# The up projection by seven block products in tiles of 512 tokens, with every transform ahead of the feed-forward

## The chip, the cores and the metric

One Trainium2 chip, one NeuronCore. The metric is the device time of one execution in microseconds. TensorE (PE) multiplies, VectorE (DVE), ScalarE (ACT) and GpSimd (POOL) work on its results, SyncE (SP) issues nearly all transfers.

## What is computed

```
def _attn_ref(x, w_r, w_i, b_r, b_i):          # x: 8 x 3072 x 256
    X = np.fft.rfft(x, axis=1)
    Yr = Xr @ w_r - Xi @ w_i + b_r
    Yi = Xr @ w_i + Xi @ w_r + b_i
    Yr, Yi = soft-shrink by 0.01
    return np.fft.irfft(Yr + 1j * Yi, n=3072, axis=1)

def _moe_ref(x, w_in, w_out):                  # 24576 x 256, 256 x 2048, 2048 x 256
    h = x @ w_in
    g = np.where(h >= 1, h, np.where(h <= -1, 0, (h + 1) ** 2 / 4))
    return g @ w_out
```

The weights of the feed-forward come as float64; all else is float32. To keep float32's accuracy with the faster matmul format (F32R), an operand is held as two rounded parts, hi and lo, and a product is three matmuls: hi x hi, lo x hi, hi x lo.

## The kernel before

The transform of length 3072 = 48 x 64 is done as matmuls in four stages. The first stage runs over "halves" of x (96 partitions x 2 columns of j x 256 channels, 128 of them): load_x, split_x_hi (ACT), split_x_lo (DVE), stage1 (three matmuls of 512 columns), store_z to a DRAM scratch. The second stage, the mixing of channels and the inverse's first stage run over 96 "units" of two frequency groups (12 per batch): load_z, stage2, split_X, planes, mix (24 matmuls of 256 columns), shrink, split_Y, stage3 (12 matmuls of 256 columns), store_u to a second DRAM scratch. The inverse's last stage, load_u and stage4 (L309), writes y transposed (channels on the partitions) as yth and ytl.

The feed-forward runs over 64 tiles of 384 tokens and 16 blocks of 128 hidden channels, 1024 steps. up (L324) is six matmuls of 384 columns (two halves of the channels, three parts each) into one PSUM bank; then the gate: ACT's Relu r (L329), DVE's min and multiply (L331) and max (L333). split_g makes gh on ACT (L340) and gl on DVE (L341). down (L357) follows three steps later, nine matmuls of 256 columns that add into two PSUM banks over a tile's 16 steps; after a tile's last one ot is copied and stored.

The order is written out by hand (manual_schedule): each engine runs its instructions in program order. First come 22 halves, then a loop over the units of six batches with the first stage's halves and the weight conversion spread through it (weight_steps: float64 bits to two parts, on DVE, ACT and POOL). The feed-forward then starts, and the 24 units of the last two batches run between its steps, one every eight steps (the list `extra`). stage4 of the next tile runs after steps 3 and 11 of a tile.

```
        for n in range(N + DELTA):
            if n < N:
                up(n)
            if 1 <= n <= N:
                split_g(n - 1)
            for e, a in extra.get(n, ()):
                e(*a)
            if i + 1 < NX and f in (3, 11):
                stage4(i + 1, 0 if f == 3 else 1)
            if n >= DELTA:
                down(n - DELTA)
```

Of the kernel before, what the change touches and what calls it, by code (L numbers as in the profile page):

```python
# [71 lines left out]
def round_r(a):  # L72
    """To 11 mantissa bits, nearest even."""
# [21 lines left out]
def tile_fft_mix_moe(  # L95
# [9 lines left out]
    TOK = JT * Q  # L105
    NS = TOK // P
    NU = G // 2
    DELTA = 3

    const = ctx.enter_context(tc.tile_pool(name="const", bufs=1))  # L110
    work = ctx.enter_context(tc.tile_pool(name="work", bufs=2))
    psum = ctx.enter_context(tc.tile_pool(name="psum", bufs=2, space=bass.MemoryType.PSUM))
    dram = ctx.enter_context(tc.tile_pool(name="dram", bufs=1, space=bass.MemoryType.DRAM))

    xv = x.rearrange("b (q j) d -> b q j d", j=J)
    ov = out.rearrange("(b t r j) e -> b j r t e", b=B, t=NS, j=J)
# [21 lines left out]
    xin, xs, zst = {}, {}, {}  # L138
    HT = JT // 2
# [323 lines left out]
    with tc.manual_schedule():  # L463
# [48 lines left out]
        for u in range(U1):  # L512
# [5 lines left out]
            if u >= 3:  # L518
                store_u(u - 3)
# [121 lines left out]
```

## Time and profile before

| | |
|---|---|
| median of 3 runs | 2840.24 us (2839.85 to 2841.37) |
| span of the profiled execution | 2840.5 us |
| PE busy | 2816.6 us, 99% |
| DVE busy | 2140.1 us, 75% |
| ACT busy | 1464.3 us, 52% |
| POOL busy | 139.7 us, 5% |
| up products begin | at 440.7 us |

The profile shows one execution. Busy time is the time in which an engine has an instruction under way; matmuls overlap, so their cost is read from start to start of neighbours and not from their length. The chain that ended last follows the work back from the last instruction, at each step to what released it. A row of the timeline is one instruction (or some alike in a row): start, length, engine, line, operation, tiles and shapes, and in brackets how long its engine was idle before it and what ended that.

### The profile page before, as it was taken

To read this page: it belongs to the slowest core of one execution; us is meant where nothing else is said; L and a number is where in the kernel's file an instruction comes from. 1 tells how busy PE (TensorE), PEld (TensorE's weight loads), DVE (VectorE), ACT (ScalarE), POOL (GpSimd) and SP (SyncE) were. 2 spreads that over 40 slices of the span, in tenths; PEclk is the share of its full clock that TensorE was granted. 3 is DMA by queue.
4 is the path that set the end of the run, shared out by engine and by line. 5 is a ranking of instruction groups with operands and counts; after the bars stand their busy time and mean duration, and the time that the engine had idled before them with its cause. 6 is when DMAs were issued, how large, how long until landed. Compare 5 with 4: busy or idle time off the path is not lost.

```text
span 2840.5 us, 53099 instructions
## 1 busy us (share of the span) xinstructions
PE 2816.6 (99%) x20416; PEld 2774.8 (98%) x20416; DVE 2140.1 (75%) x4084; ACT 1464.3 (52%) x3034; POOL 139.7 (5%) x137
## 2 busy tenths in 40 slices
PE   7999999999999999999999999999999999999999
PEld 5999999999999999999999999999999999999999
DVE  5898987777777777777777777777777777777776
ACT  5777775554454444444444444444444444444444
POOL 0333330000000000000000000000000000000000
PEclk9999999999999999999999999999999999999999
DMA  8877772211111000000000000000000000000000
GB/s 250 253 218 214 219 208 90 67 47 43 40 40 53 29 22 23 23 23 23 23 23 23 23 23 23 23 23 23 23 23 23 24 23 23 23 23 23 23 24 18
DMA packets 110009, 168.43 MB, mean 59 GB/s; under 512 B 11099, under 2 KB 85691, under 8 KB 109755
## 3 DMA queue, kind: packets, MB, share of 16 engines
q1 hardware_dynamic: 108554, 161.82, 18.9%
q8 instruction: 160, 2.62, 0.4%
q0 software_dynamic: 1200, 3.22, 0.4%
q14 instruction: 95, 0.77, 0.1%
HBM read 89.50 MB, written 75.50 MB: 58 GB/s over the span
## 4 chain that ended last, share of the span: by engine, by line
PE 95%; DVE 3%; ACT 1%; DMA 1%; issue 1%; ACTq 0%; DVEq 0%; SPq 0%; POOLq 0%
PE acc L357 38%; PE ps_h L324 38%; PE ps_mix L242 8%; PE ps_i L309 4%; PE ps_f L169 3%; PE ps_f L190 2%; PE ps_i L277 2%; DVE xl L159 1%; DVE yl L268 1%; ACT xh L154 1%; DVE Xl L208 0%; DMA z_d<-zst 0%; ACT Xh L207 0%; ACT ust L285 0%; DMA c_sb<-in_c 0%
## 5 line engine op out<-in xcount | busy, mean ns | idle before, releaser
L329 ACT ACTIVATE r<-ps_h,half 128x384 f32<-128x384 f32 x1024 | 595.5, 582 | 1169.2 <-PE ps_h L324 1152.7
L331 DVE SCALAR_TENSOR_TENSOR sq<-r 128x384 f32<-128x384 f32 x1024 | 571.5, 558 | 568.6 <-ACT r L329 558.2
L357 PE MATMUL acc<-wouth,gh 128*128 128x256 f32 x3072 | 872.3, 284 | 0.0
L357 PE MATMUL acc<-wouth,gl 128*128 128x256 f32 x3072 | 864.2, 281 | 0.0
L357 PE MATMUL acc<-woutl,gh 128*128 128x256 f32 x3072 | 859.1, 280 | 0.0
L324 PE MATMUL ps_h<-yth,winl 128*128 128x384 f32 x2048 | 692.1, 338 | 0.0
L324 PE MATMUL ps_h<-yth,winh 128*128 128x384 f32 x2048 | 690.4, 337 | 0.4 <-ACT yth L311 0.4
L324 PE MATMUL ps_h<-ytl,winh 128*128 128x384 f32 x2048 | 690.0, 337 | 0.1
L333 DVE TENSOR_TENSOR g<-ps_h,sq 128x384 f32<-128x384 f32 x1024 | 570.9, 558 | 35.6
L357 PEld LDWEIGHTS acc<-wouth,gh 128*128 128x128 f32 x3072 | 578.6, 188 | 0.8
L357 PEld LDWEIGHTS acc<-woutl,gh 128*128 128x128 f32 x3072 | 577.5, 188 | 0.5
L357 PEld LDWEIGHTS acc<-wouth,gl 128*128 128x128 f32 x3072 | 577.2, 188 | 0.2 <-DVE gl L341 0.2
L341 DVE TENSOR_TENSOR gl<-g,gh 128x384 fp32r<-128x384 f32 x1024 | 561.5, 548 | 0.2 <-ACT gh L340 0.2
L340 ACT CAST gh<-g 128x384 fp32r<-128x384 f32 x1024 | 516.2, 504 | 12.1 <-DVE g L333 12.1
L324 PEld LDWEIGHTS ps_h<-yth,winh 128*128 128x128 f32 x2048 | 385.9, 188 | 0.8 <-ACT yth L311 0.8
L324 PEld LDWEIGHTS ps_h<-ytl,winh 128*128 128x128 f32 x2048 | 384.6, 188 | 0.4 <-DVE ytl L312 0.4
L324 PEld LDWEIGHTS ps_h<-yth,winl 128*128 128x128 f32 x2048 | 384.1, 188 | 0.0
L309 PE MATMUL ps_i<-c_sb,uin 96*128 96x96 f32 x1024 | 131.6, 271 | 0.0
L309 PEld LDWEIGHTS ps_i<-c_sb,uin 96*128 96x128 f32 x1024 | 131.2, 191 | 0.0
L170 ACT COPY zst<-ps_f 96x512 f32<-96x512 f32 x121 | 70.6, 583 | 106.6 <-PE ps_f L169 98.4
L242 PE MATMUL ps_mix<-wm_rh,Xh 128*128 128x256 f32 x384 | 114.0, 297 | 0.0
L242 PE MATMUL ps_mix<-wm_rh,Xl 128*128 128x256 f32 x384 | 108.4, 282 | 0.0
(74 smaller groups left out, 2693.3 us busy)
## 6 DMA issues: line engine op xcount, KB each, us to landing
xin<-in_x SPq DMA_DIRECT2D x64, 384.0 KB, 4.2
z_d<-zst SPq DMA_DIRECT2D x64, 384.0 KB, 4.0
zin<-z_d SPq DMA_DIRECT2D x96, 256.0 KB, 4.0
u_d<-ust SPq DMA_DIRECT2D x96, 256.0 KB, 2.8
uin<-u_d SPq DMA_DIRECT2D x64, 384.0 KB, 3.8
out<-ot SPq DMA_DIRECT2D x256, 96.0 KB, 2.0
wraw<-in_moe_w_in SPq DMA_DIRECT2D x16, 256.0 KB, 3.9
wraw<-in_moe_w_out SPq DMA_DIRECT2D x16, 256.0 KB, 4.1
```

The lines of the kernel that those rows point to most:

```text
L169: nc.tensor.matmul(ps[:Q], lhsT=c1_sb[:, w, :], rhs=mv, start=k == 0, stop=k == 2)
L170: copy(zst[i][:, r * HT : (r + 1) * HT, :], ps[:Q])
L190: nc.tensor.matmul(ps[:, gi, d].rearrange("p c s -> p (c s)"), lhsT=z[:, gi, d * P : (d + 1) * P], rhs=t_sb[:, 2 * v + gi, :], start=True, ...
L242: nc.tensor.matmul(ps[:, gi, :], lhsT=a, rhs=wm[nm, k][:, d, :], start=n == 0, stop=n == 6 * ND - 1)
L309: nc.tensor.matmul(ps[:, jj, :], lhsT=a[:, jj, d * P : (d + 1) * P], rhs=c2_sb, start=True, stop=True)
L324: nc.tensor.matmul(ps, lhsT=win[w][:, d, f * P : (f + 1) * P], rhs=mv[:, d].rearrange("p q j -> p (q j)"), start=k == 0, stop=k == 3 * ND - 1)
L329: nc.scalar.activation(r, ps, AF.Relu, bias=half, scale=0.5)
L331: nc.vector.scalar_tensor_tensor(out=sq, in0=r, scalar=1.0, in1=r, op0=ALU.min, op1=ALU.mult)
L333: nc.vector.tensor_tensor(out=g, in0=ps, in1=sq, op=ALU.max)
L340: nc.scalar.copy(gh, g)
L341: nc.vector.tensor_tensor(out=gl, in0=g, in1=gh.bitcast(F32), op=ALU.subtract)
L357: nc.tensor.matmul(o, lhsT=a[:, s * P : (s + 1) * P], rhs=wout[w][:, f, :], start=f == 0 and k == 0 and s != 1, stop=f == NF - 1 and k == ...
```

## The change

The up projection works on tiles of 512 tokens and on pairs of blocks of 128 hidden channels (p, eight pairs). The channels make 2 halves, the tokens 2 halves, the pair 2 blocks: eight block products, which Strassen's form (in Winograd's variant) replaces by seven. The seven weight combinations are made once when the weights are converted (split_weights, on POOL), the four sums of y per tile on POOL (prep_sums), and their split into hi and lo on ACT and DVE in three parts of 256, 512 and 1024 columns (prep_split), during units 4, 5 and 6 of the tile before. A unit (tile, pair) has seven products of three matmuls of 256 columns, which add into four quarters X, V, Y, Z of two PSUM banks; X is added to three times, and after each the running sum is copied out by ACT (snap). DVE adds the copies to Y, V, Z (sum_second, sum_first) to make the four blocks of h, 128 x 1024.

The gate is Relu (ramp) and Square on ACT over 1024 columns, and one DVE instruction (gate: h clamped from below at 1, then the smaller of that and the square); split_hi and split_lo are over 1024 columns too. The down products are the same matmuls, in eight pieces of three, spread between the seven products, three units late.

All 96 units of the transforms run in the loop ahead of the feed-forward; the first eight stage4 pieces run in its last four steps, the rest inside the feed-forward, eight for every 24 units. x is loaded and z stored by halves. SBUF pools are released on the way: that of the first stage at unit 84, that of the units ahead of the feed-forward, and the feed-forward's buffers lie in the room set free.

```diff
-    TOK = JT * Q
-    NS = TOK // P
...
+    NP = NF // 2
...
+    JH = J // 2
+    QT = 32
+    NK = Q // QT
+    TH = QT * JH // 2
+    NS = 2 * TH // P
+    NHB = 2 * B
+    NT = NHB * NK
+    NUNIT = NT * NP
...
+    left = lambda name, **k: tc.alloc_tile_pool(name=name, bufs=1, side="left", reuse_waits="tile", **k)
...
+    def load_x(h):
+        b, m = divmod(h, 2 * NJ)
+        xin[h] = first_st.tile([Q, HT, D], F32, tag="xin", bufs=5, name="xin")
...
-    def up(n):
-        i, f = divmod(n, NF)
-        hi, lo = yt[i] if f < NF - 1 else yt.pop(i)
-        ps = psum.tile([P, TOK], F32, tag="C", bufs=3, name="ps_h")
-        k = 0
-        for d in range(ND):
-            for w, mv in ((0, hi), (0, lo), (1, hi)):
-                nc.tensor.matmul(
-                    ps, lhsT=win[w][:, d, f * P : (f + 1) * P], rhs=mv[:, d].rearrange("p q j -> p (q j)"), start=k == 0, stop=k == 3 * ND - 1
-                )
-                k += 1
-        r = work.tile([P, TOK], F32, tag="ya", name="r")
-        nc.scalar.activation(r, ps, AF.Relu, bias=half, scale=0.5)
-        sq = work.tile([P, TOK], F32, tag="yb", bufs=1, name="sq")
-        nc.vector.scalar_tensor_tensor(out=sq, in0=r, scalar=1.0, in1=r, op0=ALU.min, op1=ALU.mult)
-        g = work.tile([P, TOK], F32, tag="yc", name="g")
-        nc.vector.tensor_tensor(out=g, in0=ps, in1=sq, op=ALU.max)
-        gp[n] = g
...
+        v3, r3 = (a.rearrange("p (f c) -> p f c", f=2) for a in (vf, rf))
+
+        if d == 0:
+            wpair[p] = first_st.tile([P, 8, P], F32, tag="wpair", name="wpair")
+        a = wpair[p]
+        nc.gpsimd.tensor_tensor(out=a[:, 0::7, :] if d == 0 else a[:, 1:3, :], in0=v3, in1=r3, op=ALU.add)
+        if d == 0:
+            return
+        del wpair[p]
+        for to, i, j, op in (
+            (3, 7, 2, ALU.add),
+            (4, 3, 0, ALU.subtract),
+            (5, 0, 7, ALU.subtract),
+            (6, 1, 4, ALU.subtract),
+        ):
+            nc.gpsimd.tensor_tensor(out=a[:, to, :], in0=a[:, i, :], in1=a[:, j, :], op=op)
+        hi, lo = (w[:, p] for w in win)
+        nc.scalar.copy(hi, a[:, 0:7, :])
+        nc.gpsimd.tensor_tensor(out=lo, in0=a[:, 0:7, :], in1=hi.bitcast(F32), op=ALU.subtract)
...
+    def stage4(c, d):
+        hb, m = divmod(c, JH // JT)
+        a = uin[c] if d < ND - 1 else uin.pop(c)
+        if m == 0 and d == 0:
+            yt[hb] = pools["in"].tile([P, ND, Q, JH], F32, tag="yt", bufs=2, name="yt")
+        ps = psum.tile([P, JT, Q], F32, tag="D", bufs=3, name="ps_i2")
+        for jj in range(JT):
+            nc.tensor.matmul(ps[:, jj, :], lhsT=a[:, jj, d * P : (d + 1) * P], rhs=c2_sb, start=True, stop=True)
+        nc.scalar.copy(yt[hb][:, d, :, m * JT : (m + 1) * JT], ps.rearrange("p j q -> p q j"))
+    ops, raw_t = {}, {}
+    def halves_of(i):
+        hb, k = divmod(i, NK)
+        y = yt[hb]
+        return [[y[:, d, k * QT + t * QT // 2 : k * QT + (t + 1) * QT // 2, :] for t in range(2)] for d in range(ND)]
+    def prep_sums(i):
+        (b11, b12), (b21, b22) = halves_of(i)
+        t = raw_t[i] = pools["ff"].tile([P, 4, QT // 2, JH], F32, tag="tsum", name="tsum")
+        for to, a, b in ((0, b12, b11), (2, b22, b12), (1, b22, t[:, 0]), (3, b21, t[:, 1])):
+            nc.gpsimd.tensor_tensor(out=t[:, to], in0=a, in1=b, op=ALU.subtract)
+    def prep_split(i, part):
+        if part == 0:
+            ops[i] = [pools["ff"].tile([P, 7, TH], F32R, tag=f"op{k}", bufs=2, name=f"op{k}") for k in "hl"]
+        hi, lo = ops[i]
+        hb, k = divmod(i, NK)
+        if part == 0:
+            sl, src = slice(0, 1), halves_of(i)[0][0].rearrange("p q j -> p (q j)")
+            hi, lo = (a[:, 0, :] for a in (hi, lo))
+        elif part == 1:
+            src = yt[hb][:, 1, k * QT : (k + 1) * QT, :].rearrange("p q j -> p (q j)")
+            hi, lo = (a[:, 1:3, :].rearrange("p o n -> p (o n)") for a in (hi, lo))
+        else:
+            src = raw_t.pop(i).rearrange("p o q j -> p (o q j)")
+            hi, lo = (a[:, 3:7, :].rearrange("p o n -> p (o n)") for a in (hi, lo))
+        nc.scalar.copy(hi, src)
+        nc.vector.tensor_tensor(out=lo, in0=src, in1=hi.bitcast(F32), op=ALU.subtract)
+        if part == 2 and k == NK - 1:
+            del yt[hb]
+    ups, snaps, hs, rs, gs, acc = {}, {}, {}, {}, {}, {}
+    FACTORS = ((0, 0), (1, 1), (6, 2), (2, 6), (3, 3), (4, 4), (5, 5))
+    def product(n, which, to, start):
+        i, p = divmod(n, NP)
+        if n not in ups:
+            ups[n] = [
+                psum.tile([P, 2, TH], F32, tag="C", bufs=3, name="ps_yz"),
+                psum.tile([P, 2, TH], F32, tag="D", bufs=3, name="ps_xv"),
+            ]
+        ps = ups[n]["YZXV".index(to) // 2][:, "YZXV".index(to) % 2, :]
+        w, m = FACTORS[which - 1]
+        hi, lo = ops[i]
+        for k, (a, mv) in enumerate(((0, hi), (0, lo), (1, hi))):
+            nc.tensor.matmul(
+                ps, lhsT=win[a][:, p, w, :], rhs=mv[:, m, :], start=start and k == 0, stop=k == 2, skip_group_check=True
+            )
+    def snap(n, at):
+        if n not in snaps:
+            snaps[n] = pools["ff"].tile([P, 3, TH], F32, tag="snap", bufs=2, name="snap")
+        nc.scalar.copy(snaps[n][:, at, :], ups[n][1][:, 0, :])
+    def sum_second(n):
+        h = hs[n] = pools["ff"].tile([P, 4, TH], F32, tag="h", bufs=3, name="h")
+        yz, xv = ups[n]
+        u3 = snaps[n][:, 2, :]
+        nc.vector.tensor_tensor(out=h[:, 2, :], in0=yz[:, 0, :], in1=u3, op=ALU.add)
+        nc.vector.tensor_tensor(out=h[:, 3, :], in0=xv[:, 1, :], in1=u3, op=ALU.add)
+    def sum_first(n):
+        yz, xv = ups.pop(n)
+        nc.vector.tensor_tensor(out=hs[n][:, 0:2, :], in0=yz, in1=snaps.pop(n)[:, 0:2, :], op=ALU.add)
+    def ramp(n):
+        r = rs[n] = pools["ff"].tile([P, 4, TH], F32, tag="r", bufs=2, name="r")
+        nc.scalar.activation(r, hs[n], AF.Relu, bias=half, scale=0.5)
+    def square(n):
+        nc.scalar.activation(rs[n], rs[n], AF.Square)
+    def gate(n):
+        nc.vector.scalar_tensor_tensor(out=hs[n], in0=hs[n], scalar=1.0, in1=rs.pop(n), op0=ALU.max, op1=ALU.min)
+    def split_hi(n):
+        gh = pools["ff"].tile([P, 4, TH], F32R, tag="gh", bufs=2, name="gh")
+        nc.scalar.copy(gh, hs[n])
+        gs[n] = gh
+    def split_lo(n):
+        gl = pools["ff"].tile([P, 4, TH], F32R, tag="gl", bufs=2, name="gl")
+        gh = gs[n]
+        nc.vector.tensor_tensor(out=gl, in0=hs.pop(n), in1=gh.bitcast(F32), op=ALU.subtract)
+        gs[n] = gh, gl
...
+    def finish_tile(i):
+        hb, k = divmod(i, NK)
+        b, m = divmod(hb, 2)
+        ot = pools["ff"].tile([P, NS, D], F32, tag="ot", name="ot")
+        a0, a1 = acc.pop(i)
+        nc.scalar.copy(ot[:, 0:2, :], a0)
+        nc.vector.tensor_copy(ot[:, 2:4, :], a1)
+        for s in range(NS):
+            q = k * QT + s * P // JH
+            nc.sync.dma_start(ov[b, m, q : q + P // JH], ot[:, s, :])
...
+        for u in range(UN + 3):
...
+            if u == 84:
+                for _ in ws:
+                    pass
+                first_st.release()
+                pools["in"] = right("in")
...
+            if u >= UN - 1:
+                for c, d in [x for x in (next(four, None), next(four, None)) if x]:
+                    stage4(c, d)
+                    if d == 1 and c + 2 < NHB * JH // JT:
+                        load_u(c + 2)
+            if 2 <= u < UN + 2:
+                stage3(u - 2)
+        fold.release()
+        pools["ff"] = left("ff")
+        prep_sums(0)
+        for part in range(3):
+            prep_split(0, part)
+        LAG = 3
+        NG = ND * JH // JT
+        for n in range(NUNIT + LAG):
+            i, p = divmod(n, NP)
+            hb, k = divmod(i, NK)
+            live = n < NUNIT
+            d_n = n - LAG
+            def D_(*pieces):
+                for j in pieces:
+                    down(d_n, j)
+            if live:
+                product(n, 1, "X", True)
+                product(n, 5, "Y", True)
+                product(n, 2, "Z", False)
+                snap(n, 1)
+            if 1 <= n <= NUNIT:
+                sum_first(n - 1)
+            if 2 <= n <= NUNIT + 1:
+                split_hi(n - 2)
+            D_(0)
+            if live:
+                product(n, 6, "X", False)
+                snap(n, 0)
+            if 2 <= n <= NUNIT + 1:
+                split_lo(n - 2)
+            if 1 <= n <= NUNIT:
+                ramp(n - 1)
+            D_(1, 2, 3)
+            if live:
+                product(n, 7, "X", False)
+                product(n, 4, "V", False)
+                snap(n, 2)
+                sum_second(n)
+            if 1 <= n <= NUNIT:
+                square(n - 1)
+            D_(4, 5)
+            if live and hb + 1 < NHB:
+                at = [g * 5 // 2 for g in range(NG)]
+                if k * NP + p in at:
+                    c, d = divmod(at.index(k * NP + p), ND)
+                    c += (hb + 1) * (JH // JT)
+                    stage4(c, d)
+                    if d == ND - 1 and c + 2 < NHB * JH // JT:
+                        load_u(c + 2)
+            if live and i + 1 < NT:
+                if p == 3:
+                    prep_sums(i + 1)
+                if p in (4, 5, 6):
+                    prep_split(i + 1, p - 4)
+            if 1 <= n <= NUNIT:
+                gate(n - 1)
+            D_(6, 7)
+            if live:
+                product(n, 3, "Y", False)
+            if d_n >= 0 and d_n % NP == NP - 1:
+                finish_tile(d_n // NP)
+        pools["ff"].release()
+        pools["in"].release()
```

## Rows read from the trace of the kernel before

**Rows 1.** The page: busy us, share of the span and instructions by engine.
```profile
PE 2816.6 (99%) x20416; PEld 2774.8 (98%) x20416; DVE 2140.1 (75%) x4084; ACT 1464.3 (52%) x3034; POOL 139.7 (5%) x137
```

**Rows 2.** The page: chain that ended last, by line, shares of the span.
```profile
PE acc L357 38%; PE ps_h L324 38%; PE ps_mix L242 8%; PE ps_i L309 4%; PE ps_f L169 3%; PE ps_f L190 2%; PE ps_i L277 2%; DVE xl L159 1%; DVE yl L268 1%; ACT xh L154 1%; DVE Xl L208 0%; DMA z_d<-zst 0%; ACT Xh L207 0%; ACT ust L285 0%; DMA c_sb<-in_c 0%
```

**Rows 3.** Windows: length, busy PE PEld DVE ACT POOL, clock, DMA share, GB/s.
```profile
200.00:300.00 100.00, 99.56 (x771) 93.79 (x770) 89.84 (x173) 72.48 (x159) 38.08 (x32) 1.00 0.73 217
1500.00:2000.00 500.00, 500.00 (x3602) 500.00 (x3601) 373.93 (x718) 239.05 (x493) 0.00 (x0) 1.00 0.08 23
```

**Rows 4.** Timeline (start us, length us): one feed-forward step.
```profile
1499.91 0.34 PE L324 MATMUL ps_h<-yth,winh 128*128 128x384 f32 x1
...
1500.97 0.28 PE L357 MATMUL acc<-wouth,gh 128*128 128x256 f32 x1
...
1501.23 0.58 ACT L329 ACTIVATE r<-ps_h,half 128x384 f32<-128x384 f32 x1 [1.14 <-PE ps_h L324]
...
1502.03 0.34 PE L324 MATMUL ps_h<-yth,winh 128*128 128x384 f32 x1
```

**Rows 5.** Timeline: a stage4 piece and the matmul behind it.
```profile
517.03 1.03 PE L309 MATMUL ps_i<-c_sb,uin 96*128 96x96 f32 x8
...
517.84 0.36 PE L357 MATMUL acc<-wouth,gh 128*128 128x256 f32 x1
```

**Rows 6.** Groups by shape on ACT: busy us, mean ns, idle before.
```profile
L426 ACT CAST winh<-val 128x256 fp32r<-128x256 f32 x16 | 6.6, 414 | 0.0
...
L267 ACT CAST yh<-y 128x512 fp32r<-128x512 f32 x96 | 59.9, 624 | 40.2 <-DVE y L260 39.2
...
L311 ACT CAST yth<-ps_i 128x384 fp32r<-128x384 f32 x128 | 61.7, 482 | 26.7 <-PE ps_i L309 26.7
...
L285 ACT COPY ust<-ps_i 128x512 f32<-128x512 f32 x96 | 55.7, 580 | 0.0
...
L329 ACT ACTIVATE r<-ps_h,half 128x384 f32<-128x384 f32 x1024 | 595.5, 582 | 1169.2 <-PE ps_h L324 1152.7 <-DVE yl L268 13.3 <-DVE sq L331 0.8
```

**Rows 7.** Groups by shape on DVE, two inputs.
```profile
L251 DVE TENSOR_TENSOR y<-ps_mix,bias 128x256 f32<-128x256 f32 x16 | 5.9, 411 | 2.0 <-PE ps_mix L242 2.0
...
L260 DVE TENSOR_TENSOR y<-y,yc 128x512 f32<-128x512 f32 x96 | 65.6, 683 | 1.1
...
L268 DVE TENSOR_TENSOR yl<-y,yh 128x512 fp32r<-128x512 f32 x96 | 82.6, 860 | 0.0
```

**Rows 8.** Timeline: a POOL subtraction and a DVE one that met it.
```profile
306.07 1.06 POOL L428 TENSOR_TENSOR woutl<-val,rest 128x256 fp32r<-128x256 f32 x1
...
306.47 1.22 DVE L268 TENSOR_TENSOR yl<-y,yh 128x512 fp32r<-128x512 f32 x1
```

**Rows 9.** Timeline: neighbours on ACT and on DVE without a wait.
```profile
600.32 0.58 ACT L329 ACTIVATE r<-ps_h,half 128x384 f32<-128x384 f32 x1 [0.41 <-PE ps_h L324]
600.80 0.50 ACT L340 CAST gh<-g 128x384 fp32r<-128x384 f32 x1
...
600.20 0.56 DVE L333 TENSOR_TENSOR g<-ps_h,sq 128x384 f32<-128x384 f32 x1
600.67 0.55 DVE L341 TENSOR_TENSOR gl<-g,gh 128x384 fp32r<-128x384 f32 x1
```

**Rows 10.** Timeline: PE waiting for ACT and restarting; ACT waiting for DVE.
```profile
441.38 0.48 ACT L311 CAST yth<-ps_i 128x384 fp32r<-128x384 f32 x1
...
441.91 0.45 PE L324 MATMUL ps_h<-yth,winh 128*128 128x384 f32 x1 [0.44 <-ACT yth L311]
...
442.50 0.44 PE L324 MATMUL ps_h<-ytl,winh 128*128 128x384 f32 x1
...
442.79 0.33 PE L324 MATMUL ps_h<-yth,winl 128*128 128x384 f32 x1
...
2831.56 0.56 DVE L333 TENSOR_TENSOR g<-ps_h,sq 128x384 f32<-128x384 f32 x1
...
2832.22 0.51 ACT L340 CAST gh<-g 128x384 fp32r<-128x384 f32 x1 [0.89 <-DVE g L333]
```

More of the change, by code (lines that the diff above doesn't have):

```diff
@@ L180, in load_z @@
         b, v = divmod(u, NU)
-        zin[u] = work.tile([P, 2, D], F32, tag="zin", bufs=3, name="zin")
+        zin[u] = fold.tile([P, 2, D], F32, tag="zin", bufs=3, name="zin")
         nc.sync.dma_start(zin[u], zg[b][:, 2 * v : 2 * v + 2, :])
@@ L247, in shrink @@
         ps = yp[u]
-        y = work.tile([P, 2, D], F32, tag="ya", name="y")
+        y = fold.tile([P, 2, D], F32, tag="ya", bufs=2, name="y")
         if v == 0:
@@ L256, in shrink @@
         between()
-        c = work.tile([P, 2, D], F32, tag="yb", bufs=1, name="yc")
+        c = fold.tile([P, 2, D], F32, tag="yb", name="yc")
         nc.vector.tensor_scalar(out=c, in0=y, scalar1=-LAM, scalar2=LAM, op0=ALU.max, op1=ALU.min)
@@ L279, in stage3 @@
                 )
-        ust[u] = ps
-    def evac_u(u):
-        ps = ust[u]
-        ust[u] = work.tile([P, 2, D], F32, tag="ust", name="ust")
+        ust[u] = fold.tile([P, 2, D], F32, tag="ust", bufs=2, name="ust")
         nc.scalar.copy(ust[u], ps)
@@ new lines, in split_hi, with down @@
+    def split_hi(n):
[7 more added lines that the diff above has]
+        gs[n] = gh, gl
+    def down(n, piece):
+        if n < 0 or n >= NUNIT:
+            return
+        i, p = divmod(n, NP)
+        fi, s = divmod(piece, NS)
+        if p == 0 and piece == 0:
+            acc[i] = [psum.tile([P, 2, D], F32, tag=k, bufs=1, name=f"acc{k}") for k in "AB"]
+        gh, gl = gs[n]
+        o = acc[i][s // 2][:, s % 2, :]
+        f = 2 * p + fi
+        blk, at = 2 * fi + 1 - s // 2, (s % 2) * P
+        for k, (a, w) in enumerate(((gh, 0), (gh, 1), (gl, 0))):
+            nc.tensor.matmul(
+                o,
+                lhsT=a[:, blk, at : at + P],
+                rhs=wout[w][:, f, :],
+                start=f == 0 and k == 0 and s % 2 == 0,
+                stop=f == NF - 1 and k == 2,
+                skip_group_check=True,
+            )
+        if piece == 2 * NS - 1:
+            del gs[n]
@@ new lines, in finish_tile, with halves @@
+    def finish_tile(i):
[8 more added lines that the diff above has]
+            nc.sync.dma_start(ov[b, m, q : q + P // JH], ot[:, s, :])
+    UN = B * NU
+    LEAD = 6
+    def halves(u):
+        lo, hi = (min(NH, 2 * NJ + LEAD + 4 * k // 3) for k in (u, u + 1))
+        return range(lo, hi)
@@ L465, in tile_fft_mix_moe @@
         nc.gpsimd.dma_start(c1_sb, c1)
-        load_x(1)
-        load_x(2)
+        for h in range(1, 5):
+            load_x(h)
         nc.vector.memset(half, 0.5)
@@ L471, in tile_fft_mix_moe @@
         for n, w in (("r", w_r), ("i", w_i)):
-            st = work.tile([P, ND, D], F32, tag="ya", name=f"wm_st{n}")
+            st = fold.tile([P, ND, D], F32, tag="ya", bufs=2, name=f"wm_st{n}")
             wst.append((n, st, w.rearrange("(d p) e -> p d e", p=P)))
@@ L544, in tile_fft_mix_moe @@
-            if u >= 2:
-                stage3(u - 2)
-                evac_u(u - 2)
-            if u == U1 - 4:
+            if u == 84:
[3 more added lines that the diff above has]
+                pools["in"] = right("in")
                 load_u(0)
                 load_u(1)
-            if u in (U1 - 2, U1 - 1):
-                stage4(0, u - U1 + 2)
-        for _ in ws:
-            pass
-        while 2 * (stored + 1) <= halves(U1).start:
-            store_z(stored)
-            stored += 1
@@ L603, in tile_fft_mix_moe @@
[L603 to L617 removed]
+            if 1 <= u < UN + 1:
+                shrink(u - 1, more_weights if 2 <= u < 84 else lambda: None)
```

325 lines of the change are left out of this document (104 added, 221 removed).

## The prediction

> **What bounds the kernel now.** I read the busy shares first: TensorE (PE) 99%, VectorE (DVE) 75%, ScalarE (ACT) 52% [rows 1]. Then the chain that ended last by line: 38% down products (L357), 38% up products (L324), the rest nearly all transform matmuls [rows 2]. Then two stretches, since a mean mixes stages: in the transforms ahead of the feed-forward PE is busy 99.6 of 100 us with DVE at 89.8, and inside the feed-forward 500 of 500 us with DVE at 374 and ACT at 239 [rows 3]. So both stages are paced by PE, and fewer columns on PE are worth their full price as long as no other engine's order comes to the front. Last I read one feed-forward step in time: six up matmuls of 384 columns take 1.06 us, nine down matmuls of 256 columns the next 1.06 us [rows 4]: 0.1767 and 0.1178 us each, 0.46 ns a column for both widths.
>
> **Step 1, the products.** Before: 1024 steps x 6 x 0.1767 = 1085.6 us of up products. After: 48 tiles x 8 units = 384 units x 7 products x 3 matmuls of 256 columns = 8064 x 0.1178 = 949.9 us. Down is 9216 matmuls of 256 columns before and after. All are on the path: -135.7 us. The Trainium skill (TensorE: Matmul & The Clock Gate, Back-to-back issue gap) gives columns / 2.4 GHz + 2.5 ns, so by it 162.5 and 109.2 ns and an estimated saving of 118 us; [rows 4] show 8% more than that for both widths, so the rows decide. I take -135.7.
>
> **Step 2, the load of the other engines.** Prices. ACT from SBUF: 0.41 us for 256 columns, 0.62 for 512 [rows 6], so 1.04 for 1024 by the same slope; from PSUM 0.48 for 384 and 0.58 for 512, so 0.38 for 256; a bias tile adds 0.10 (L329 against L311, both 384 from PSUM), so the Relu of 1024 takes 1.14. DVE, two inputs: 0.41 for 256, 0.68 for 512 [rows 7], so 1.22 for 1024. An instruction that waits for nothing starts 0.10 us before the one in front of it ends on ACT, 0.09 on DVE [rows 9]. Per unit ACT gets three snaps, ramp, square and split_hi, 4.4 us of durations, and with its shares of prep_split, stage4 and finish_tile 4.9; DVE gets sums, gate and split_lo, 3.9, and with its shares 4.3. A unit's PE work is 45 x 0.1178 = 5.30 us, plus a third of a stage4 (0.81 us each, [rows 5]): 5.57. On average PE still has most to do.
>
> **Step 3, the order, which is what decides.** PE, ACT and DVE each run in program order. Time from a unit's first matmul; three matmuls are a group of 0.353. Product 4 ends after ten groups, 3.53; ACT starts 0.26 after the last matmul before it (from 1500.97 to 1501.23, [rows 4]): snap 2 at 3.79 to 4.17, square 4.07 to 5.11, gate 5.15 to 6.37 on DVE, then split_hi of the next unit 0.10 later (2831.56 + 0.56 to 2832.22, [rows 10]), 6.47 to 7.51, and behind it in ACT's queue snap 0, 7.41 to 7.79. Product 7 adds into the X that snap 0 reads, so PE waits for it; PE goes on 0.05 after ACT (441.38 + 0.48 to 441.91, [rows 10]), 7.84. Without any wait PE reaches product 7 at 5.30 + 2.82 = 8.12. So an ordinary unit is free of stalls, with 0.28 to spare.
>
> In units 4, 5 and 6 of a tile, prep_split stands between square and gate: its copy on ACT behind square, its subtraction on DVE ahead of gate. Queued behind that subtraction are gate, behind gate split_hi, behind that snap 0, and for snap 0 waits PE. The gate moves by both durations less 0.18 of overlap:
> - unit 4 (256 columns): 0.41 + 0.41 - 0.18 = 0.64, less the spare 0.28: 0.36 us
> - unit 5 (512): 0.62 + 0.68 - 0.18 = 1.12, stall 0.84
> - unit 6 (1024): 1.04 + 1.22 - 0.18 = 2.08, stall 1.80
>
> After the stall the rest of the unit shifts with PE, so nothing adds up over units. A restart of PE costs 0.11 more (0.29 instead of 0.176 to the next matmul, [rows 10]): 3.00 + 0.33 a tile. In two tiles of three one of these units also runs a stage4, which gives PE 0.81 of other work and delays the prep copy by 0.67: less 0.09 on average. So 3.24 us x 47 tiles = +152 us. Bounds: latencies and the extrapolated 1024-column prices may be off by 0.15 us down or 0.2 up in each of 141 such units: 131 to 180.
>
> **Step 4, prep_sums on GpSimd (POOL).** Four subtractions of 256 columns a tile, 1.06 us each [rows 8]. POOL has nothing else in its queue, so they run as soon as their buffer is free, right after unit 6's prep. There they meet DVE: a two-input SBUF operation that met a POOL one took 1.22 us instead of 0.68 [rows 8, 7], and L268, which meets them often, has a mean of 860 against 683 ns at L260 [rows 7]. The Trainium skill (SBUF — State Buffer, two separate sides) calls the shared port pair an exclusive lock; by it all four could hold DVE 4.2 us a tile, an estimated 199 us if each blocked the path. By the timetable one delays split_lo (0.14 us reaches PE) and one the next gate (0.19): +0.33 at most behind a stall; I take +10 us, bounds 0 and 30.
>
> **Step 5, the seam and the ends.** The transforms of the last two batches are the same matmuls before as inside the feed-forward; the stretch ahead holds PE at 99.6% with weight conversion beside it [rows 3], and these units have none: 0. At the seam nothing covers: after the last stage4 its copy (0.26 + 0.48), four POOL subtractions in a row (4 x 1.1), the 1024-column copy and subtraction (1.04 + 1.22) come before product 5 can run through: about 7.5 us without PE, and before it the last unit's stage3 waits some 0.6 for its split and buffers laid over the folded pools may come free 1.2 late: +10. The loads and stores of the moved transforms go ahead on SP with them; in the feed-forward SP then holds only u loads and output stores. Units 0 to 2 have no down products to hide under; by the timetable they take 13.7 us for 7.4 of PE work: +6. At the end the last unit's chain (sum, ramp, square, gate, split: 7.2 us) outlasts the down products left: +1. Together +17, bounds 10 and 25. Output stores fall from 256 to 192 issues: 0.
>
> **Step 6, the first stage by halves and the weight fold.** Twice as many x loads and z stores pass SP in the stretch ahead; DMA is at a share of 0.73 there [rows 3] and PE is the bound, so 0 to +10. The fold adds POOL work for eight pairs of weight chunks, its longest an 896-column subtraction of some 3.7 us (3.5 x 1.06), beside a DVE that is 90% busy: 0 to +15 if it blocks DVE each time. I take +3 for both, bounds -5 and 20.
>
> **Sum.** 2840.5 (span; the median of the runs is 2840.24, so nothing lies around it) - 135.7 + 152 + 10 + 17 + 3 = 2887 us. The case's own range by the bounds: 2705 + 131 + 0 + 10 - 5 = 2841 to 2705 + 180 + 30 + 25 + 20 = 2960.
>
> **Rivals.**
> - The preparation is hidden. ACT at 4.9 and DVE at 4.3 of 5.57 us have room on average, and the 0.28 us to spare rests on extrapolated prices. If the chain square, prep, gate, split, snap 0 does not reach PE, steps 3 and 4 fall out: 2840.5 - 135.7 + 17 + 3 = 2725 us, faster by 4%. Break-even lies at 116 us of stalls, 2.5 us a tile. Against it: the three engines' order leaves prep_split no other place. Chance 0.20, part of it for halfway cases up to 2835.
> - Every unit stalls. If square takes a bias tile as the Relu does (+0.10) and the 1024-column prices are 0.1 higher each (square, gate, split_hi), the chain is 0.4 longer, 0.12 more than the spare: 243 ordinary units x (0.12 + 0.11) = 56 us, and the 141 prep units pay the whole 0.4, 56 us more: about 3000. It decides from a chain of 4.59 us between product 4 and the next product 7. Chance 0.10.
> - The seven products do not come at the down products' price, since up now changes weights every 256 columns as well. Nine down matmuls in a row do just that at 0.1178 [rows 4], and the change from up to down shows no gap. Each 0.01 us would cost 81 us. Chance 0.03.
>
> **How the numbers follow.** The forecast has 0.65, the rest (0.02) is scattered. A measurement of this kernel can tell 0.2% (5.7 us) from no change. Of the forecast's 0.65 about 0.58 lies above 2846, 0.05 within, 0.02 below; with the rivals: slower 0.69, same 0.06, faster 0.25. To hold 8 in 10 the range has to reach into the first rival: 2735 to 2960; the likeliest case's own is 2841 to 2960.
>
> **What would show it.** In the trace after: product 7 (PE on ps_xv) waiting for snap's copy on ACT some 140 times, 0.4 to 1.9 us each, three per tile and none in other units; 256-column up matmuls 0.118 us apart; a gap of some 7 us on PE at the feed-forward's start; PE's share down to about 94%. The prediction is wrong if PE waits at other products, if ordinary units wait too, or if units 4 to 6 of a tile are as long as the others.

## The result and the profile after

The changed kernel takes 2879.93 us (median of 4 runs, 2879.82 to 2880.91), the kernel before 2840.72 us on the same chip: ratio 1.0138, 95% interval 1.0123 to 1.0152. The forecast was 2887.0 (2735 to 2960). The profiled execution has a span of 2878.1 us, 37.6 more than before.

First the page: busy us by engine, the chain that ended last by engine and by line, and the groups of the feed-forward (count, busy us, mean ns, then idle time before them and its releaser).

```profile
PE 2754.2 (96%) x22336; PEld 2682.6 (93%) x22336; DVE 2053.2 (71%) x2932; ACT 2103.8 (73%) x3410; POOL 369.1 (13%) x353
...
PE 71%; ACT 17%; DVE 10%; DMA 1%; issue 1%; SPq 0%; POOL 0%; ACTq 0%; POOLq 0%
...
L460 ACT COPY snap<-ps_xv 128x256 f32<-128x256 f32 x1152 | 427.3, 371 | 331.3 <-PE ps_xv L453 319.8
L492 DVE TENSOR_TENSOR gl<-h,gh 128x1024 fp32r<-128x1024 f32 x384 | 473.6, 1233 | 221.0 <-ACT gh L486 221.0
L486 ACT CAST gh<-h 128x1024 fp32r<-128x1024 f32 x384 | 403.2, 1050 | 207.9 <-DVE h L482 191.7
L453 PE MATMUL ps_xv<-oph,winh 128*128 128x256 f32 x1536 | 447.3, 291 | 93.2 <-ACT snap L460 91.7
L482 DVE SCALAR_TENSOR_TENSOR h<-h,r 128x1024 f32<-128x1024 f32 x384 | 469.4, 1222 | 50.0 <-ACT r L479 50.0
L476 ACT ACTIVATE r<-h,half 128x1024 f32<-128x1024 f32 x384 | 443.5, 1155 | 0.0
...
L479 ACT ACTIVATE r<-r 128x1024 f32<-128x1024 f32 x384 | 408.3, 1063 | 0.0
```

PE is 62 us less busy than before [rows 1], and the span is longer all the same. The chain says why: of it 17% lies on ACT and 10% on DVE, where before nearly all of it was PE lines [rows 2]. The only matmul group of the feed-forward with idle time to speak of is the first one into ps_xv (products 1, 6, 7 and 4 share this row), and what ends that idle time is the snap on ACT.

The waits of PE say the same (us in total, times, longest us). A wait is credited from where the trace has the last matmul end, so it is shorter than the gap between two starts.

```profile
PE ps_xv L453 <- ACT snap L460: 91.7, 97, 1.5
PE ps_f L177 <- ACT xh L164: 7.0, 3, 3.6
```

One such wait in time, behind a tile's unit 6 (start us, length us; timeline of all engines):

```profile
1475.50 1.04 ACT L430 CAST oph<-tsum 128x1024 fp32r<-128x1024 f32 x1
...
1476.57 1.22 DVE L431 TENSOR_TENSOR opl<-tsum,oph 128x1024 fp32r<-128x1024 f32 x1 [1.14 <-ACT oph L430]
...
1477.72 1.22 DVE L482 SCALAR_TENSOR_TENSOR h<-h,r 128x1024 f32<-128x1024 f32 x1
...
1477.88 2.32 POOL L413 TENSOR_TENSOR tsum<-yt 128x256 f32<-128x256 f32 x2 [43.26 <-DVE opl L431]
...
1478.60 0.28 PE L507 MATMUL accB<-wouth,gl 128*128 128x256 f32 x1
...
1478.96 1.05 ACT L486 CAST gh<-h 128x1024 fp32r<-128x1024 f32 x1 [2.15 <-DVE h L482]
1479.92 0.36 ACT L460 COPY snap<-ps_xv 128x256 f32<-128x256 f32 x1
...
1480.33 0.38 PE L453 MATMUL ps_xv<-oph,winh 128*128 128x256 f32 x1 [1.46 <-ACT snap L460]
```

Read it downwards: the preparation's copy on ACT, its subtraction on DVE, behind that the gate, behind that split_hi (gh) on ACT, behind that snap 0, and only then product 7. ACT stands idle for 2.15 us with the snap, whose data are long there, queued behind gh; PE stands from 1478.72 (the start at 1478.60 and the 0.12 us that one matmul takes) to 1480.33.

By the starts of all matmuls, an ordinary unit takes 5.35 us and one with a stage4 6.24. The units behind units 4, 5 and 6 stall 0.18, 0.61 and 1.62 us at product 7, with some 0.1 each for the restart, in 126 of 141 places (in the other 15 a stage4 stands beside unit 4's piece and covers it); no other product waits. Where the 37.6 us come from, start to start, in groups of matmuls:

| | forecast | measured |
|---|---|---|
| up products (step 1) | -135.7 | -124.8 (1076.9 to 952.1) |
| stalls at product 7 (step 3) | +152 | +125.0 |
| POOL against DVE (step 4) | +10 | 0, by an experiment below |
| seam and ends (step 5) | +17 | +10.5 seam, +0.8 behind the last matmul |
| first stage's gaps and first matmul (step 6) | +3 | +4.1, -1.4 |
| transforms, same matmuls | 0 | +5.0 (125.8 to 127.1 ns each) |
| down products, same 9216 matmuls | 0 | +17.8 (117.8 to 119.7 ns each), -1.1 in gaps |
| stage4 | 0 | +1.7 |
| sum | +46.3 | +37.6 |

### The profile page after: what moved, and what is told of

It reads as the page before. It is cut to its first block, busy times and chain, and to the rows that moved or that the text cites. A ratio compares the mean times of both kernels' runs of the same rounds, so it can differ in the third digit from the quotient of the medians.

```text
span 2878.1 us, 54084 instructions
## 1 busy us (share of the span) xinstructions
PE 2754.2 (96%) x22336; PEld 2682.6 (93%) x22336; DVE 2053.2 (71%) x2932; ACT 2103.8 (73%) x3410; POOL 369.1 (13%) x353
## 4 chain that ended last, share of the span: by engine, by line
PE 71%; ACT 17%; DVE 10%; DMA 1%; issue 1%; SPq 0%; POOL 0%; ACTq 0%; POOLq 0%
PE ps_xv L453 15%; PE accA L507 14%; PE accB L507 13%; PE ps_yz L453 10%; PE ps_mix L247 9%; DVE h L482 5%; ACT gh L486 5%; PE ps_i L397 4%; DVE opl L431 4%; ACT r L479 3%; ACT r L476 3%; PE ps_f L198 3%; ACT oph L430 3%; PE ps_f L177 3%; ACT snap L460 2%; PE ps_i L284 2%
## 5 line engine op out<-in xcount | busy, mean ns | idle before, releaser
L492 DVE TENSOR_TENSOR gl<-h,gh 128x1024 fp32r<-128x1024 f32 x384 | 473.6, 1233 | 221.0 <-ACT gh L486 221.0
L486 ACT CAST gh<-h 128x1024 fp32r<-128x1024 f32 x384 | 403.2, 1050 | 207.9 <-DVE h L482 191.7
L453 PE MATMUL ps_xv<-oph,winh 128*128 128x256 f32 x1536 | 447.3, 291 | 93.2 <-ACT snap L460 91.7
L482 DVE SCALAR_TENSOR_TENSOR h<-h,r 128x1024 f32<-128x1024 f32 x384 | 469.4, 1222 | 50.0 <-ACT r L479 50.0
L476 ACT ACTIVATE r<-h,half 128x1024 f32<-128x1024 f32 x384 | 443.5, 1155 | 0.0
L507 PE MATMUL accB<-wouth,gh 128*128 128x256 f32 x1536 | 442.6, 288 | 0.0
L507 PE MATMUL accA<-wouth,gh 128*128 128x256 f32 x1536 | 435.2, 283 | 0.4 <-ACT gh L486 0.4
L507 PE MATMUL accA<-wouth,gl 128*128 128x256 f32 x1536 | 432.4, 281 | 0.9 <-DVE gl L492 0.9
L507 PE MATMUL accB<-wouth,gl 128*128 128x256 f32 x1536 | 432.3, 281 | 0.0
L507 PE MATMUL accB<-woutl,gh 128*128 128x256 f32 x1536 | 431.9, 281 | 0.0
L453 PE MATMUL ps_xv<-oph,winl 128*128 128x256 f32 x1536 | 431.7, 281 | 0.0
L479 ACT ACTIVATE r<-r 128x1024 f32<-128x1024 f32 x384 | 408.3, 1063 | 0.0
```

The lines of the kernel that those rows point to most:

```text
L453: nc.tensor.matmul(ps, lhsT=win[a][:, p, w, :], rhs=mv[:, m, :], start=start and k == 0, stop=k == 2, skip_group_check=True)
L476: nc.scalar.activation(r, hs[n], AF.Relu, bias=half, scale=0.5)
L479: nc.scalar.activation(rs[n], rs[n], AF.Square)
L482: nc.vector.scalar_tensor_tensor(out=hs[n], in0=hs[n], scalar=1.0, in1=rs.pop(n), op0=ALU.max, op1=ALU.min)
L486: nc.scalar.copy(gh, hs[n])
L492: nc.vector.tensor_tensor(out=gl, in0=hs.pop(n), in1=gh.bitcast(F32), op=ALU.subtract)
```

## The experiments

Two theories stood at the start. **The order**: what costs is that prep_split's subtraction, which waits for its copy on ACT, stands ahead of the gate in DVE's queue; put it elsewhere and the 125 us go. **The port**: POOL's sums hold DVE, and that feeds the stalls. A third question came up with the table: why the same down products became 1.6% dearer.

**The gate ahead of the preparation.** Two blocks of the loop change places. The gate runs on DVE, so only DVE's order changes: the three copies a tile keep their place on ACT.

```
+            if 1 <= n <= NUNIT:
+                gate(n - 1)
             if live and i + 1 < NT:
                 if p == 3:
                     prep_sums(i + 1)
                 if p in (4, 5, 6):
                     prep_split(i + 1, p - 4)
-            if 1 <= n <= NUNIT:
-                gate(n - 1)
```

> Undoes the order alone: gate stands ahead of prep_sums and prep_split in the program, all else as in the changed kernel. Order theory: gate then ends 1.22 us after square's end whatever prep does, split_hi and snap 0 of the next unit come in time, and the subtraction of prep_split delays only sum_first, which has room. The 125 us in which PE waits for snap at product 7 go: 2880 - 125 = 2755 us, the waits of PE for snap fall from 92 us to under 5. Work theory (the copies and subtractions of prep_split do not fit beside a unit's other work on ACT and DVE, wherever they stand): PE waits at another product instead, 2850 us or more.

2754.62 us (2753.46 to 2755.33), ratio 0.9697, interval 0.9681 to 0.9714. Its page, by engine, and the chain, and what is left of PE's waits for a snap:

```profile
PE 2718.0 (99%) x22336; PEld 2673.3 (97%) x22336; DVE 2054.0 (75%) x2932; ACT 2103.5 (76%) x3410; POOL 367.3 (13%) x353
...
PE 95%; DVE 1%; DMA 1%; ACT 1%; issue 0%; SPq 0%; POOL 0%; ACTq 0%; POOLq 0%
...
PE ps_xv L453 <- ACT snap L460: 2.0, 3, 1.0
```

All stalls in steady state are gone and every unit is 5.35 or 6.24 us long, with each instruction still there. The price lay in the place of three subtractions a tile on DVE, not in the work of the preparation.

**No preparation at all** (all products read the first tile's operands).

```
-        hi, lo = ops[i]
+        hi, lo = ops[0]
...
-            if live and i + 1 < NT:
-                if p == 3:
-                    prep_sums(i + 1)
-                if p in (4, 5, 6):
-                    prep_split(i + 1, p - 4)
```

> Leaves out the sums and the hi and lo parts of y for every tile but the first: all tiles multiply the first tile's operands. Everything else runs. Order theory: the same 2755 us as with gate ahead of prep_split, within 5 us, since there the preparation is hidden whole. Work theory: well below the run with gate first, by up to 100 us, since the work itself has the price. It also gives the floor without preparation: ordinary units of 5.35 us, the seam of some 13 us and the end left as they are.

2753.88 us (2752.9 to 2755.67), ratio 0.9695 (0.9681 to 0.971). The same as with the gate first: behind the gate the preparation costs nothing that can be measured.

**No sums on POOL**, the port theory's own test (later tiles use the first tile's sums).

```
         prep_sums(0)
+        t_first = [raw_t[0]]
...
                 if p == 3:
-                    prep_sums(i + 1)
+                    raw_t[i + 1] = t_first[0]
```

> Leaves out prep_sums on GpSimd for every tile but the first: the later tiles split the first tile's four sums. Port theory (step 4 of the forecast): DVE no longer meets POOL, 10 us less, 2870 us (0 to 30 less). Order theory after the trace of the changed kernel, in which the DVE instructions beside POOL's are no longer than others: within 3 us of 2880.

2880.11 us (2879.87 to 2882.45), ratio 1.0139 (1.0124 to 1.0154), POOL's busy time down from 369.1 to 165.0 us. The time of the changed kernel is unmoved, so the port theory falls for it and step 4's term was 0.

**The preparation in seven equal pieces**, one of 256 columns in each of units 1 to 7, still ahead of the gate (prep_piece does for 256 columns what prep_split does); the sums move to unit 1.

```
-                if p == 3:
+                if p == 1:
                     prep_sums(i + 1)
-                if p in (4, 5, 6):
-                    prep_split(i + 1, p - 4)
+                if p >= 1:
+                    prep_piece(i + 1, p - 1)
```

> The same preparation in seven pieces of 256 columns, one in each of units 1 to 7 of a tile, at the same place between square and gate (prep_sums two units earlier). Order theory: a stall is what a piece's copy and subtraction exceed the spare of about 0.5 us by: as unit 4 shows now, 0.17 and a restart of 0.1, and nearly nothing where the unit has a stage4 (7 of 21 in three tiles). 14 x 0.27 + 7 x 0.03 = 4.0 us instead of 8.0 for three tiles: 16 x 4.0 = 64 us less, 2816 us. Work theory: four copies and four subtractions more a tile, some 0.2 us of fixed cost each: 2880 us or up to 2950.

2848.71 us (2847.11 to 2850.64), ratio 1.0027 (1.0016 to 1.0039): 31 less than the changed kernel, where about 64 were expected. A piece in a unit without a stage4 costs 0.28 us, as worked out. Beside a stage4 it costs 0.14 instead of 0.03, and one piece in 24 units costs 1.0. The timeline of this last, with an undisturbed piece behind it:

```profile
1389.72 0.74 POOL L413 TENSOR_TENSOR tsum<-yt 128x256 f32<-128x256 f32 x1 [9.30 <-ACT yt L398]
1389.98 0.76 DVE L444 TENSOR_TENSOR opl<-yt,oph 128x256 fp32r<-128x256 f32 x1 [1.23 <-ACT oph L443]
1390.42 2.60 POOL L413 TENSOR_TENSOR tsum<-yt,tsum 128x256 f32<-128x256 f32 x2
...
1390.66 1.75 DVE L497 SCALAR_TENSOR_TENSOR h<-h,r 128x1024 f32<-128x1024 f32 x1
...
1393.82 0.39 PE L468 MATMUL ps_xv<-oph,winh 128*128 128x256 f32 x1 [0.75 <-ACT snap L475]
...
1396.49 0.42 DVE L444 TENSOR_TENSOR opl<-yt,oph 128x256 fp32r<-128x256 f32 x1 [0.50 <-ACT oph L443]
...
1396.83 1.22 DVE L497 SCALAR_TENSOR_TENSOR h<-h,r 128x1024 f32<-128x1024 f32 x1
```

Here POOL's sums wait for a stage4's copy and start just as the piece and the gate do: 0.76 instead of 0.42 us and 1.75 instead of 1.22. That is step 4's effect, at the size of [rows 8], on the path. In the changed kernel the sums start behind the last piece, 0.16 us after the gate (1477.88 and 1477.72 in the timeline above); the gate takes its 1.22, POOL is the one that takes longer, and nothing on the path is lost. So the port is a matter of who starts first, and the expectation failed because I had moved the sums without pricing where they land.

**The snap ahead of split_hi** on ACT. If snap 0 need not queue behind split_hi, product 7 can't wait for the gate.

```
-            if 2 <= n <= NUNIT + 1:
-                split_hi(n - 2)
             D_(0)
             if live:
                 product(n, 6, "X", False)
                 snap(n, 0)
             if 2 <= n <= NUNIT + 1:
+                split_hi(n - 2)
+            if 2 <= n <= NUNIT + 1:
                 split_lo(n - 2)
```

> On ACT, snap 0 stands ahead of split_hi instead of behind it. Order theory: product 7 never waits for snap 0 again; but split_hi, ramp and snap 2 now come 0.5 us later in every unit, and PE waits at product 3 for the sum that reads Y: 0.26 us in an ordinary unit, 0.4 behind unit 5 and 1.3 behind unit 6. Per tile 5 x 0.26 + 0.26 + 0.38 + 1.34 = 3.3 us instead of 2.7: 2880 + 29 = 2909 us (2890 to 2925), the waits moved from ps_xv to ps_yz. Work theory: the same work, 2880 us, at the same place.

2851.25 us (2850.74 to 2851.91), ratio 1.0038 (1.0023 to 1.0053): 29 less, where 29 more were expected. The mechanism was as expected, the price not. The wait leaves product 7 and comes back at product 3, which needs the Y that sum_second reads; on PE's weight loads (waits, as above):

```profile
PEld ps_yz L453 <- DVE h L467: 80.9, 295, 1.3
```

An ordinary unit takes 5.58 us (+0.23 against 0.26 worked out). What the expectation left out are the 8 of 24 units with a stage4: its 0.89 us of PE work stands between snap 2 and product 3 and hides the wait, so those units pay nothing. The units behind units 5 and 6 cost 0.36 us and 0.43 (with a stage4) to 1.33 (without), restart included. Moving the instruction traded a rare long wait for a frequent short one.

**The transforms ahead, alone**: the kernel before, with all 96 units ahead of the feed-forward.

```
-    U1 = (B - 2) * NU
+    U1 = UN
...
-            load_z(u + 2)
+            if u + 2 < UN:
+                load_z(u + 2)
...
-        for k in range(2):
-            at(2 + k, split_x_lo, halves(U1).start + k)
```

> One part of the change alone, in the kernel before: all 96 units of the transforms run in the loop ahead of the feed-forward, none between its steps; up, gate and tiles of 384 tokens stay. Forecast (step 5): the same matmuls at the same price, 0 for the moved units, and a seam that the old feed-forward covers with less: 2841 us, up to 2848. Rival: the move has a price of its own (units without first-stage halves are paced by DVE or ACT, or loads come late): 2850 us or more.

2839.6 us (2838.46 to 2841.61), ratio 0.9994 (0.9985 to 1.0004). Step 5's zero for the moved transforms holds, and their matmuls are 125.9 ns apart there: the 127.1 of the changed kernel doesn't come from where they run.

**Gate first, and the first tile's sums on DVE.** At the seam, where the feed-forward starts, POOL does four sums in a row, and DVE has little else to do. Beside the exchange of the gate:

```
-    def prep_sums(i):
+    def prep_sums(i, eng=None):
...
-            nc.gpsimd.tensor_tensor(out=t[:, to], in0=a, in1=b, op=ALU.subtract)
+            (eng or nc.gpsimd).tensor_tensor(out=t[:, to], in0=a, in1=b, op=ALU.subtract)
...
-        prep_sums(0)
+        prep_sums(0, nc.vector)
```

> Gate ahead of prep_split, and the first tile's four sums on DVE instead of GpSimd. At the seam nothing else runs, so four subtractions of 0.42 us take the place of four of 1.1: 2.7 us less than with gate first alone, 2752 us if that is at 2755. If something else is late at the seam (the store that the buffers wait for), no change.

2752.19 us (2751.08 to 2753.07), ratio 0.9687 (0.9672 to 0.9701). Against the gate first alone, unit 0 takes 9.62 us instead of 11.16 and unit 1 4.68 instead of 5.59: about 2.4 us, near the 2.7 expected.

**Where the tiles lie.** Down's extra 1.9 ns did not depend on which instruction of ACT, DVE or POOL ran beside a matmul. What else had changed is the allocation: win is larger, the transforms' tiles are folded in. Two kernels built on the last one shift tiles by unused padding. The first has 128 bytes ahead of win and 128 behind half:

```
+    keep.tile([P, 32], F32, name="pad0")
     win = [keep.tile([P, NP, 7, P], F32R, name=f"win{k}") for k in "hl"]
...
     half = keep.tile([P, 1], F32, name="half")
+    keep.tile([P, 32], F32, name="pad1")
```

> The version with gate first and the seam's sums on DVE, with 128 bytes of padding ahead of win and 128 behind half: win and wout start on a multiple of 256 bytes, as in the kernel before, and the operands' place moves by 256. If the 119.7 ns of a down product (117.8 before) come from where the weights lie against 256 bytes, down goes back to 117.8, 17 us off 2752: 2735. If they don't, 2752 and 119.7 as it was.

2732.78 us (2731.47 to 2737.16), ratio 0.9624 (0.9608 to 0.964): down at 118.0 ns, up at 117.2, as expected for down.

The second has 1152 bytes ahead of wout alone:

```
+    keep.tile([P, 288], F32, name="pad0")
     wout = [keep.tile([P, NF, D], F32R, name=f"wout{k}") for k in "hl"]
```

> The same version with 1152 bytes of padding between win and wout alone: wout starts at 1280 past a multiple of 2048, as in the kernel before, and every later tile moves by 1152 with it, while win stays. If wout's place against 2048 bytes sets the down product's 119.7 ns, 117.8 and 2735 us. If the place plays no part, 2752.

2746.37 us (2744.65 to 2747.6), ratio 0.9666 (0.9652 to 0.9681): down stays at 119.7 with wout at the very place (against 2048 bytes) that it has before, but up goes to 116.9. So neither theory of wout alone holds. What fits all four layouts is the distance from the stationary to the moving operand, against 256 bytes. In bytes modulo 256, worked out from the allocation, and the mean spacing measured:

```
                    down: wout - gh, gl      up: op (yt) - win     mix: wm - X
before              224   117.8 ns           32   (384 columns)    224   125.8 ns
after, gate first    96   119.7, 119.6       160  118.1 ns           0   127.1
128 bytes twice     224   118.0               32  117.2              0   127.1
1152 bytes           96   119.7               32  116.9              0   127.1
```

(The last pair of columns is the mean of all transform matmuls; in stage3 yh lies 32 ahead of ti_sb where the table has 224, and at 0 where it has 0.) This was made up from four results, so it was put to three new kernels, one of them the changed kernel itself. The first line below, which all three have, shifts the operands, gh and gl by 128 bytes and leaves the weights where they were; the first kernel has nothing else. The second has the other line too, 32 bytes within the transforms' pool. The third is the changed kernel with the first line alone.

```
     half = keep.tile([P, 1], F32, name="half")
+    keep.tile([P, 32], F32, name="pad1")
...
     bias0 = fold.tile([P, D], F32, name="bias0")
+    fold.tile([P, 8], F32, name="pad2")
```

> The version with gate first and the seam's sums on DVE, with 128 bytes of padding behind half alone: win and wout stay where they were (128 past a multiple of 256), every operand, gh and gl move by 128. Theory of the distance: what counts is the distance between moving and stationary operand against 256 bytes; down then has 224 as in the kernel before (96 in the changed kernel) and up 32 (160 in the changed kernel), so down 118.0 ns, up 117.2, 2733 us as with padding on both sides. Rival, the place of each tile by itself: wout at 128 past 256 gives 119.7 as before, 2752; win and operands by themselves likewise 118.1.

2729.26 us (2727.28 to 2729.91), ratio 0.9605 (0.959 to 0.9619): down 117.9 ns, up 117.2. The weights had not moved, so it is not their own place. Nor is it the operands' own: gh and gl lie at the same place against 256 bytes here and in the kernel with 1152 bytes, and there down took 119.7. The page's line of engines for the kernel without the padding (gate first, sums on DVE), and with it:

```profile
PE 2717.0 (99%) x22336; PEld 2672.7 (97%) x22336; DVE 2052.9 (75%) x2936; ACT 2104.4 (77%) x3410; POOL 364.5 (13%) x349
```

```profile
PE 2695.8 (99%) x22336; PEld 2651.4 (97%) x22336; DVE 2054.0 (75%) x2936; ACT 2103.3 (77%) x3410; POOL 369.0 (14%) x349
```

The same 22336 matmuls, and PE needs 21 us less for them. An ordinary unit of the changed kernel and of this one, from product 1 to the next product 1 (timelines): 5.35 and 5.29 us.

```profile
1452.68 0.28 PE L453 MATMUL ps_xv<-oph,winh 128*128 128x256 f32 x1
...
1458.03 0.28 PE L453 MATMUL ps_xv<-oph,winh 128*128 128x256 f32 x1
```

```profile
1456.69 0.28 PE L454 MATMUL ps_xv<-oph,winh 128*128 128x256 f32 x1
...
1461.98 0.28 PE L454 MATMUL ps_xv<-oph,winh 128*128 128x256 f32 x1
```

> The same with 32 bytes more in the fold pool, behind bias0, so that zin, X, yh and yl lie 32 past the weights that they meet (wm, ti_sb), as in the kernel before; in the changed kernel the distance is 0 there. By the theory of the distance the transforms' mean spacing goes from 127.1 to 125.9 ns, 5 us less than the other kernel of this pair: 2728. By the rival no difference between the two.

2726.21 us (2725.15 to 2727.49), ratio 0.9595 (0.9579 to 0.9611), the lowest time of this study. By the times alone it can't be told from the one before; the transforms' spacing went from 127.1 to 125.9 ns as expected, and the busy time of PE by 5.8 us:

```profile
PE 2690.0 (99%) x22336; PEld 2645.6 (97%) x22336; DVE 2053.2 (75%) x2936; ACT 2105.0 (77%) x3410; POOL 367.1 (13%) x349
```

> The changed kernel itself with the 128 bytes behind half and nothing else. By the theory of the distance its products give back 15.7 us (9215 x 1.7 ns) for down and 7.3 (8064 x 0.9 ns) for up; PE then reaches product 7 some 0.05 us earlier in each of the 125 units that wait there, 6 us of longer stalls: 2880 - 23 + 6 = 2863. By the rival 2880.

2866.42 us (2866.26 to 2867.71), ratio 1.009 (1.0074 to 1.0105). Down falls by 15.7 us and up by 6.2, but the stalls grow from 125.0 to 132.7: PE reaches product 7 earlier and finds the snap no earlier. 7.7 of 21.9 us are given back, where 6 of 23 were expected.

## Why the prediction came out as it did

The sign, the mechanism and the place were right, and the time is 7 us off; but that is smaller than the errors of its terms, which cancel by luck.

- **Step 1.** Right in kind, 10.9 us too large. 8.7 of them are the price read from a single step of before [rows 4]: 0.1767 us for 384 columns, where the mean of all 6144 is 0.1753. The rest is 118.1 ns instead of 117.8.
- **The page's rule.** The Trainium skill (TensorE: Matmul & The Clock Gate, Back-to-back issue gap) would have 162.5 and 109.2 ns by a formula that the section gives for a single matmul, without the weight load that goes with each one here. The runs show 175.3, and 117.2 to 118.1, so the rows were the better source; but the saving measured, 124.8, lies nearer to the 118 by the page than to my 135.7.
- **Step 2.** Held: ramp 1155 ns for 1140 forecast, gate 1222 for 1220, split_hi 1050 for 1040, snap 371 for 380. The square at 1063 takes no bias tile's extra, so the rival of a dearer square fell.
- **Step 3.** The chain was right link by link: product 7, three units a tile, no stall elsewhere, restart 0.1. The stalls are 0.18, 0.61 and 1.62 us for 0.36, 0.84 and 1.80. The mis-sized terms are latencies and the unit: PE to ACT takes 0.20 us, not 0.26; gate to split_hi 0.02, not 0.10; and PE comes to product 7 later, with a unit of 5.35 instead of 5.30. That is some 0.18 of the 0.18 to 0.23. In 15 places a stage4 covers the shortest stall. +125 against +152, below the low bound of 131.
- **Step 4.** The 10 us were 0: the sums run while DVE's work is not on the path. The mechanism exists, as the seven pieces show: there a gate that starts 0.24 us into POOL's sum takes 1.75. The Trainium skill (SBUF — State Buffer, SBUF: two separate sides) calls the port pair an exclusive lock, and the one that starts second waits for the other's end. The trace agrees but for some 0.15 us: the sum that the gate met ran for 0.92 us (the row at 1390.42 merges it with the next one), so 0.68 of it was left, and the gate became 0.53 longer.
- **Step 5.** The seam cost 10.5 and the end 0.8, for 17. No step had the clock, which is 2.4 of the 10.5 (below); without it the seam is half of what I took. One term too large was a sum on POOL: 1.1 us taken, where sums that meet no DVE instruction take 0.72 to 0.73; the other terms of the seam were not taken apart.
- **Step 6.** 2.7 us for 3; no run tested this term.
- **What no step had**: the same down and transform products became dearer, 17.8 and 5.0 us. I had taken their price as a constant of the shape; it depends on where the operands lie. The experiments bear this out in both directions, though not by what means.
- **Rivals.** "The preparation is hidden" fell for this kernel, and its time of 2725 us is reached by the same work once the gate goes first (2754.6), the first sums run on DVE (2752.2) and the tiles are shifted (2726.2). Against it I wrote that the order leaves prep_split no other place; a line two further down would have done.

## What to carry to other kernels

Before a side task is put into an in-order queue, look at what is queued behind it on each engine and who waits for that; placed behind the last instruction on the path instead of ahead of it, the same work cost 0 instead of 125 us here. When a change moves or resizes tiles, compare the spacing of matmuls that it did not touch: a difference there is one of layout, and a padding of 128 bytes is a cheap test. And a shorter path into a wait is partly given back: 7.7 of 21.9 us here.

## What the runs showed of the hardware

**The distance between the operands.** The same 256-column matmuls are 117.9 or 119.7 ns apart (down), 117.2 or 118.1 (up), and the transforms' mean is 125.9 or 127.1, the shorter where the moving operand lies 32 bytes ahead of or behind the stationary one, the longer where it is 96 or 0, all modulo 256. Only these distances were seen, each in products of one kind, and the reason wasn't tried. The Trainium skill (SBUF — State Buffer, SBUF: two separate sides) says that on the engines' side only the port pair of DVE and POOL causes contention; the measured difference, 23 us by 128 bytes of padding alone, is between PE's own two operands, of which that sentence says nothing, and whether it is contention no run here shows.

**The clock at the seam.** Windows of the changed kernel (length, busy us of PE, PEld, DVE, ACT and POOL, granted clock, DMA share, GB/s), the last one around the stall of 1.61 us shown above:

```profile
568.00:574.00 6.00, 2.73 (x19) 2.15 (x18) 1.89 (x2) 2.75 (x6) 3.37 (x4) 0.82 0.55 168
574.00:578.00 4.00, 2.65 (x9) 2.06 (x9) 1.23 (x1) 0.85 (x3) 2.36 (x4) 0.50 0.00 0
578.00:582.00 4.00, 3.92 (x18) 3.93 (x19) 0.76 (x2) 0.87 (x3) 0.48 (x1) 0.50 0.00 0
582.00:586.00 4.00, 2.62 (x20) 2.21 (x18) 1.23 (x3) 2.73 (x5) 0.00 (x0) 0.99 0.00 0
...
1478.00:1482.00 4.00, 2.54 (x22) 2.34 (x21) 3.02 (x4) 3.02 (x5) 3.92 (x4) 1.00 0.02 4
```

and of its timeline:

```profile
570.70 0.38 PE L453 MATMUL ps_xv<-oph,winh 128*128 128x256 f32 x1 [0.87 <-ACT oph L430]
...
574.28 0.58 PE L453 MATMUL ps_yz<-oph,winh 128*128 128x256 f32 x1 [2.27 <-ACT oph L430]
...
576.56 0.41 PE L453 MATMUL ps_yz<-oph,winl 128*128 128x256 f32 x1
576.77 0.41 PE L453 MATMUL ps_xv<-oph,winh 128*128 128x256 f32 x1
```

While PE waits for the first tile's preparation, the granted clock falls to 0.50 (1.2 GHz), and from 574 to 582 us matmuls start 0.21 us apart instead of 0.118, until it is back at 0.99. That is some 17 up matmuls by 0.095 us and a stage4 of 1.57 instead of 0.81: 2.4 us, by which the seam costs more than its waits. The stalls of 1.6 us inside the feed-forward lower no clock (1.00 in the last window).
